# A fused attention and channel-mix kernel: the first unit's softmax done tile by tile under another order list, and part of the token mix moved to ScalarE in later units

## The chip, the cores and the metric

The kernel runs on one core of a Trainium2 chip. The metric is device time in microseconds (us) of one execution. Five engines work side by side, each through its own instructions in order: TensorE (PE, matrix products), VectorE (DVE), ScalarE (ACT), GpSimd (POOL) and SyncE (SP), which here issues all DMA transfers. An engine that waits for a semaphore holds up everything behind it in its own order.

## The reference

Chunked local attention, then a channel mix on its output. All is float32; B, H, S, D = 4, 8, 768, 64, so x has 4 x 768 rows of 512.

```python
# attention, chunks of 32 queries; context 16 left, 8 right, and 8 memory keys
scores = scale * np.matmul(q_c, k_full.transpose(0, 1, 3, 2))
scores = scores - np.max(scores, axis=-1, keepdims=True)
a = np.exp(scores)
a = a / (np.sum(a, axis=-1, keepdims=True) + 1e-09)
out[:, :, c_start:c_end] = np.matmul(a, v_full)
...
# channel mix on x, the attention output as (B, S, 512)
x_prev = np.concatenate([np.zeros((B, 1, D), dtype=np.float32), x[:, :-1, :]], axis=1)
xk = mu_k * x + (1.0 - mu_k) * x_prev
xr = mu_r * x + (1.0 - mu_r) * x_prev
k = np.maximum(xk @ w_k, 0.0)
v = k * k @ w_v
r = 1.0 / (1.0 + np.exp(-(xr @ w_r)))
return (r * v).astype(np.float32)
```

## The kernel before

**Tiling.** The 3072 tokens are 24 tiles of 128 and 12 units of two tiles (256 tokens). A product of the channel mix is made of three matmuls in a rounded float32 format: the operand's high part times the weight's high part, high times low, and low times high. So every operand and every weight is split once into a high part (a rounding copy, `.hi`) and a low part (a subtraction, `.lo`).

**Operations by name.** The program is a set of named operations, put in order by a planner (`Plan.order`, lines 114 to 209). For a unit u: `qk` and `vw` load a tile's inputs (672 and 512 KB), `s` computes the scores of both tiles on TensorE (lines 418 to 433), `max`, `sub`, `exp`, `sum`, `norm` are the softmax (lines 435 to 465) on arrays of 128 x 1024. For a tile t: `t` transposes the weights of attention on TensorE into PSUM, `bd.0` and `bd.1` copy the two halves of partitions into a block-diagonal buffer `aTz` (line 497), `a` multiplies with the values (line 509), `x` copies the result into `xT` (line 524). The tracker of tiles makes `bd.1` wait for `bd.0` where they run on different engines, since both write `aTz`. `mix` forms xk and xr: for unit 0 on TensorE with two diagonal matrices of mu and 1 - mu, which ScalarE makes in `dg` (lines 341 to 348), for later units on VectorE as x_prev + mu (x - x_prev), a subtraction `df` (line 593) and four fused multiply-adds per output (line 603). `h`, `g`, `v` are the three products (lines 654, 630, 630), and from unit 3 on the last product runs in seven blocks (line 961).

**Weights.** A weight chunk `w{i}` arrives as 64-bit words (1024 KB). ScalarE makes its magnitude (`.mag`, line 376), VectorE shifts the low word (`.low`, line 379) and joins them (`.join`, line 383), then come `.hi` and `.lo` (lines 316, 318, 389). Chunks w2 to w5 are w_k, needed by `h`; w0 and w1 are w_r, needed by `g`; w6 to w9 are w_v.

**What sets the order.** A string `FIRST` (lines 47 to 64) lists the operations up to the last `v` block of unit 0 as `name@engine`; the planner takes them in that order. Behind it, it places by itself, from estimated costs and due times (`te_order`, lines 212 to 241), choosing the engine where an operation has a choice. Buffers are rings: `big` has 4 places that hold both `qk` tiles and raw weights, so a transfer may wait until an old tile was read. Where the planned order leaves TensorE idle before unit 0's first `h`, the program puts in products of zeros, `warm` (lines 1085 to 1088), one for each 0.86 us of the planned gap.

Of the kernel before, what the change touches and what calls it, by code (L numbers as in the profile page):

```python
# [52 lines left out]
bd3.1@dve vw3@dma xl0.1@dve w5.load@dma w5.mag@act w0.load@dma s2@pe max2@dve w1.load@dma qk7@dma sub2@dve w5.low@dve
w5.join@dve w0.low@dve exp2@act sum2@dve vw4@dma a2@pe a3@pe x2@act x3@act w5.hi@act w5.lo@dve h0.0@pe h0.1@pe
w1.low@dve w0.mag@act h0.2@pe h0.3@pe w1.mag@act qk6@dma w0.join@dve w0.hi@act relu0.0@act norm2@dve t4@pe bd4.0@act
relu0.1@act sq0.1@act vw5@dma sq0.0@act kh0.0@act t5@pe w0.lo@dve s3@pe g0.0@pe relu0.3@act w1.join@dve w1.hi@dve
relu0.2@act bd4.1@act bd5.1@act sq0.3@act w7.load@dma w7.mag@act bd5.0@act w1.lo@dve g0.1@pe sq0.2@act a4@pe x4@act
df1@dve kh0.1@dve mix1.1@dve xh1.1@dve w8.load@dma w8.mag@act xl1.1@dve w6.load@dma a5@pe x5@act w6.mag@act mix1.0@dve
xh1.0@dve xl1.0@pool sig0.0@act sig0.1@act max3@dve sub3@dve kl0.1@dve w7.low@dve w9.load@dma w9.low@dve w6.low@dve
w7.join@dve kh0.3@act g1.0@pe g1.1@pe h1.0@pe sig1.0@act sig1.1@act w6.join@dve kl0.0@dve kh0.2@act w9.mag@act  # L60
w9.join@dve w6.hi@act kl0.3@dve exp3@act h1.1@pe w6.lo@dve h1.2@pe relu1.1@act sq1.1@act w7.hi@act w8.low@dve
w8.join@dve h1.3@pe relu1.0@act kl0.2@dve w9.hi@act relu1.3@act w7.lo@dve sq1.0@act df2@dve w8.hi@act w8.lo@dve
# [182 lines left out]
def local_attention__then__channel_mix(  # L245
# [162 lines left out]
    def scores(u):  # L408
# [62 lines left out]
        o_s = op(f"s{u}", ("pe", 1.4), f_s, l + [prior.get("s")], new=[s1], use=qs, due=ds)  # L471
        o_m = op(f"max{u}", ("dve", 1.17), f_max, [o_s], new=[m1], use=[s1], due=ds + 4)
        o_b = op(f"sub{u}", ("dve", 1.17), f_sub, [o_m], new=[e], use=[s1, m1], due=ds + 5.5)
        o_e = op(f"exp{u}", ("act", 1.02), f_exp, [o_b], use=[e], table="exp")
        o_u = op(f"sum{u}", ("dve", 1.65, True), f_sum, [o_e], new=[m2], use=[e])
        o_n = op(f"norm{u}", either(dve=(1.14, True), pool=(2.2, True)), f_norm, [o_u], use=[e, m2])
        prior.update(s=o_s)
        return o_n, e
# [661 lines left out]
```

## Time and profile before

| What | Value |
|---|---|
| three runs | 485.79, 399.02 and 399.14 us; median 399.14 us |
| the profiled execution | 398.94 us, of which the span of the profile is 397.2 us |
| TensorE busy | 388.1 us, 98% of the span |
| VectorE busy | 323.2 us, 81% |
| ScalarE busy | 215.2 us, 54% |
| GpSimd busy | 15.9 us, 4% |
| bytes moved by DMA | 46.63 MB |

The first run of the three lies far above the other two, which agree with the profiled execution within 0.2 us. Busy shares are means over stages with different limits: the first 21 us, in which inputs and weights arrive and the first unit's softmax runs, are another regime than the rest.

### The profile page before, as it was taken

What the parts mean: (1) busy time and instruction counts of PE and PEld (TensorE: products, weight loads), DVE (VectorE), ACT (ScalarE), POOL (GpSimd) and SP (SyncE); (2) the same over time, 40 slices, a digit from 0 to 9 for tenths busy, and PEclk for the clock granted to TensorE, in tenths of its full rate; (3) what the DMA queues carried; (4) which work ended last, traced back from release to release, by engine and by line L of the source; (5) the groups of instructions that cost most, each with busy time, mean ns of one, the idle gap of its engine ahead of it and who ended that gap; (6) DMA issues with size and microseconds to landing.
All of it is one profiled execution on the core that took longest, in us unless ns stands there. A gap on an engine that the chain in (4) does not pass through costs nothing.

```text
span 397.2 us, 10852 instructions
## 1 busy us (share of the span) xinstructions
PE 388.1 (98%) x4803; PEld 357.6 (90%) x4803; DVE 323.2 (81%) x561; ACT 215.2 (54%) x340; POOL 15.9 (4%) x14
## 2 busy tenths in 40 slices
PE   7889999999999999999999999999999999999996
PEld 3579889888988989989989989989989999989995
DVE  1888989998789999789879879779779779478446
ACT  1867797714642864457457466357358364344440
POOL 2243020000010000000000000000000000000000
PEclk9999999999999999999999999999999999999999
DMA  8999894011063260142142142142130130100101
GB/s 304 412 352 355 268 362 133 8 69 39 2 229 110 102 246 3 55 151 98 55 138 110 54 174 73 54 148 99 55 109 2 53 108 2 53 2 2 54 0 53
DMA packets 13054, 46.63 MB, mean 117 GB/s; under 512 B 1488, under 2 KB 1872, under 8 KB 12496
## 3 DMA queue, kind: packets, MB, share of 16 engines
q1 hardware_dynamic: 13008, 45.95, 31.9%
q8 instruction: 37, 0.61, 0.6%
q14 instruction: 9, 0.07, 0.1%
HBM read 39.65 MB, written 6.29 MB: 116 GB/s over the span
## 4 chain that ended last, share of the span: by engine, by line
PE 93%; DVE 3%; ACT 2%; DMA 1%; issue 0%; SPq 0%; DVEq 0%
PE ph L654 33%; PE pr L630 17%; PE pv L630 8%; PE pa L961 6%; PE pb L961 6%; PE px L509 6%; PE pc L961 5%; PE s L430 4%; PE pd L961 3%; PE pt L492 3%; PE xf L562 2%; DMA qk<-in_qk_dram 1%; ACT k L346 1%; DVE sm_sb L443 1%; DVE e L447 1%; DVE o L985 0%
## 5 line engine op out<-in xcount | busy, mean ns | idle before, releaser
L654 PE MATMUL ph<-xh,wkh 128*128 128x256 f32 x384 | 106.2, 277 | 0.0
L654 PE MATMUL ph<-xl,wkh 128*128 128x256 f32 x384 | 106.0, 276 | 0.0
L654 PE MATMUL ph<-xh,wkl 128*128 128x256 f32 x384 | 106.0, 276 | 0.0
L654 PEld LDWEIGHTS ph<-xh,wkh 128*128 128x128 f32 x384 | 72.1, 188 | 0.2
L654 PEld LDWEIGHTS ph<-xl,wkh 128*128 128x128 f32 x384 | 72.1, 188 | 0.0
L654 PEld LDWEIGHTS ph<-xh,wkl 128*128 128x128 f32 x384 | 72.1, 188 | 0.0
L742 ACT ACTIVATE k<-ph 128x512 f32<-128x512 f32 x48 | 28.6, 598 | 71.9 <-PE ph L654 71.8
L917 DVE TENSOR_TENSOR khl<-k,khl 128x512 fp32r<-128x512 f32 x63 | 42.2, 687 | 25.4 <-ACT khl L316 24.4
L630 PE MATMUL pr<-wrh,xh 128*128 128x512 f32 x96 | 39.1, 408 | 0.0
L630 PE MATMUL pr<-wrl,xh 128*128 128x512 f32 x96 | 37.6, 392 | 0.0
L630 PE MATMUL pr<-wrh,xl 128*128 128x512 f32 (+1 forms) x108 | 37.6, 366 | 0.0
L316 ACT CAST khl<-k 128x512 fp32r<-128x512 f32 x43 | 26.4, 622 | 7.5 <-PE pb L961 2.5
L630 PE MATMUL pv<-wvh,khl 128*128 128x512 f32 (+1 forms) x97 | 30.3, 389 | 0.0
L749 ACT ACTIVATE k<-k 128x512 f32<-128x512 f32 x47 | 29.5, 632 | 1.3
L509 PEld LDWEIGHTS px<-aTz,vw 128*64 128x64 f32 x768 | 23.4, 138 | 3.4 <-issue 2.4
L509 PE MATMUL px<-aTz,vw 128*64 128x64 f32 x768 | 25.0, 223 | 1.1 <-DVE aTz L318 1.1
L318 DVE CAST khl<-k 128x512 fp32r<-128x512 f32 x32 | 13.1, 423 | 15.6 <-ACT k L749 15.2
L316 ACT COPY aTz<-pt 64x512 f32<-64x512 f32 x34 | 19.1, 580 | 12.0 <-PE pt L492 11.1
L701 ACT ACTIVATE sg<-pr 128x512 f32<-128x512 f32 x24 | 14.3, 599 | 19.4 <-PE pr L630 19.3
L961 PE MATMUL pc<-wtbig,khl 128*128 128x256 f32 x204 | 24.6, 276 | 0.0
L630 PEld LDWEIGHTS pr<-wrh,xl 128*128 128x128 f32 x108 | 20.3, 188 | 4.6
L961 PEld LDWEIGHTS pc<-wtbig,khl 128*128 128x128 f32 x204 | 23.8, 188 | 0.0
(110 smaller groups left out, 757.3 us busy)
## 6 DMA issues: line engine op xcount, KB each, us to landing
qk<-in_qk_dram SPq DMA_DIRECT2D x24, 672.0 KB, 6.1
vw<-in_vw_dram SPq DMA_DIRECT2D x24, 512.0 KB, 4.8
out_dram<-o SPq DMA_DIRECT2D x23, 256.0 KB, 2.1
raw<-in_w_k_dram SPq DMA_DIRECT2D x4, 1024.0 KB, 8.0
raw<-in_w_v_dram SPq DMA_DIRECT2D x4, 1024.0 KB, 6.6
raw<-in_w_r_dram SPq DMA_DIRECT2D x2, 1024.0 KB, 5.9
out_dram<-o SPq DMA_DIRECT2D x2, 128.0 KB, 1.7
id_sb<-in_ident_dram SPq DMA_DIRECT2D x1, 64.0 KB, 6.8
```

The costliest lines, as they stand in the source:

```text
L316: e.copy(dst, src)
L318: e.tensor_copy(dst, src)
L430: nc.tensor.matmul(s5[CHUNK * j : CHUNK * (j + 1), h, c, r, :], q4[z, r, j, :], k3[z, r, STEP * j : STEP * j + NK], start=True, stop=True,)
L492: nc.tensor.transpose(p[:, n * P : (n + 1) * P], e[:, n // 2, c, n % 2, :], id_sb)
L509: nc.tensor.matmul(p3[64 * h : 64 * h + 64, 2 * g : 2 * g + 2, CHUNK * j : CHUNK * j + CHUNK], v[:, g, h, j, :], a[:, h, g, j, :], start=True,
L630: nc.tensor.matmul(p[:, a : a + step], x, w[:, a : a + step], start=start, stop=stop and a + step == DM)
L654: nc.tensor.matmul(z, w, x[:, k], start=start, stop=stop)
L701: nc.scalar.activation(T["sg", u][:, c * DM : (c + 1) * DM], T["pr", u, c], AF.Sigmoid)
L742: e.activation(r, T["ph", u, f], AF.Relu)
L749: e.activation(q, q, AF.Square)
L917: e.tensor_sub(T["al", u, name], src, T["ah", u, name].bitcast(F32))
L961: nc.tensor.matmul(p, l[:, i], r[i], start=i + k == 0, stop=i == FT // 2 - 1 and k == 2)
```

## The change

Three edits.

1. **The first unit goes tile by tile.** For u = 0 the scores of the second tile go into two PSUM buffers of the tag `tp` instead of the second half of the `s` buffer, and `s`, `max`, `sub`, `exp`, `sum`, `norm` exist once for each tile; those of the second tile are named with a `b` (`s0b`, `max0b`, ...). `t0` waits for the first tile's `norm0`, `t1` for `norm0b`. In all units the mask of an edge tile is written by one memset for each head half, where it was one for both.
2. **Another list `FIRST`.** It covers the same stretch, up to the last `v` block of unit 0. It also names other engines for some operations: `norm0`, `w7.lo`, `kl0.3` and `kl1.2` go to GpSimd, `norm1` and `xl1.0` leave it.
3. **From unit 3 on, ScalarE makes (1 - mu) x_prev** (`old`, four activations of 128 x 256 for each of the two outputs), and VectorE adds mu x with its four fused operations. The subtraction `df` is gone there.

The list begins so (the rest of it is shown by the rows further down):

```diff
-qk1@dma qk0@dma s0@pe max0@dve sub0@dve mu@dma w3.load@dma w3.low@dve w3.mag@act w3.join@dve exp0@act sum0@dve id@dma
-norm0@dve dg0@act dg1@act qk2@dma qk3@dma s1@pe t0@pe t1@pe bd0.0@act vw1@dma w3.hi@dve w3.lo@pool bd1.1@act vw0@dma
...
+qk0@dma s0@pe qk1@dma max0@dve sub0@dve exp0@act s0b@pe max0b@dve mu@dma id@dma sum0@dve norm0@pool qk3@dma qk2@dma
+w3.load@dma dg1@act vw0@dma vw1@dma w2.load@dma sub0b@dve exp0b@act sum0b@dve norm0b@dve dg0@act w3.mag@act s1@pe
...
```

The rest of the code, cut to its core:

```diff
+        split = u == 0
+        parts = [[c] for c in range(QPU)] if split else [range(QPU)]
...
+        def f_s(cs):
+            if cs[0] == 0:
+                T["s", u] = ps("s", f"s{u}", QPU)
+            else:
+                for h in range(2):
+                    T["s", u, cs[0], h] = ps("tp", f"s{u}_{h}")
...
-                nc.vector.memset(s5[0:CHUNK, :, c, :, 0:LEFT], NEG)
...
+                for h in range(2):
+                    if qts[ts[c]][1] == 0:
+                        nc.vector.memset(room(h, c)[0:CHUNK, :, 0:LEFT], NEG)
...
+        for n, cs in enumerate(parts):
...
+            o_s = op(f"s{u}{v}", ("pe", 1.4 * z), on(f_s), [l[c] for c in cs] + [prior.get("s")], new=[s1] if first else t1, use=[qs[c] for c in cs], due=ds)
...
+            o_e = op(f"exp{u}{v}", ("act", 1.02 * z), on(f_exp), [o_b], use=[e], table="exp")
...
+            norms += [o_n] * len(cs)
...
-        o_t = op(f"t{t}", ("pe", 0.45), f_t, [o_n, o_id, prior.get("t")], new=[s2], use=[e], due=dt)
+        o_t = op(f"t{t}", ("pe", 0.45), f_t, [o_n[c], o_id, prior.get("t")], new=[s2], use=[e], due=dt)
...
+        if u >= FAST:
+            for m in (0, 1):
+                fs = Slot("x4", [0, 1])
...
+                    f = T["xf", u, m] = sb(fs, [P, KT, UTOK], f"xf{u}_{m}")
+                    for k in range(KT):
+                        nc.scalar.activation(
+                            f[:, k], T["xT", u][:, k, :UTOK], AF.Copy, scale=mu_sb[:, m + 2, k : k + 1]
+                        )
...
+                        nc.vector.scalar_tensor_tensor(
+                            f[:, k], T["xT", u][:, k, 1 : 1 + UTOK], mu_sb[:, m, k : k + 1], f[:, k], ALU.mult, ALU.add
+                        )
```

**How the order moved, first place: SyncE's transfers and ScalarE up to the first `bd`.** A number behind `raw` is the weight chunk, behind `qk` and `vw` the tile; the last number in a name is the buffer's own. SyncE before, from its first transfer on:

```order
L416 DMA qk1_101<-in_qk_dram 128x1344
L416 DMA qk0_103<-in_qk_dram 128x1344
L333 DMA mu_sb_65<-in_mu_dram 128x8
L360 DMA raw3_179<-in_w_k_dram 128x1024
L332 DMA id_sb_64<-in_ident_dram 128x128
L416 DMA qk2_209<-in_qk_dram 128x1344
L416 DMA qk3_211<-in_qk_dram 128x1344
L486 DMA vw1_295<-in_vw_dram 128x1024
L486 DMA vw0_300<-in_vw_dram 128x1024
L360 DMA raw2_304<-in_w_k_dram 128x1024
L360 DMA raw4_362<-in_w_k_dram 128x1024
```

SyncE of the change, the same stretch:

```order
L418 DMA qk0_101<-in_qk_dram 128x1344
L418 DMA qk1_139<-in_qk_dram 128x1344
L335 DMA mu_sb_65<-in_mu_dram 128x8
L334 DMA id_sb_64<-in_ident_dram 128x128
L418 DMA qk3_189<-in_qk_dram 128x1344
L418 DMA qk2_191<-in_qk_dram 128x1344
L362 DMA raw3_193<-in_w_k_dram 128x1024
L529 DMA vw0_204<-in_vw_dram 128x1024
L529 DMA vw1_206<-in_vw_dram 128x1024
L362 DMA raw2_208<-in_w_k_dram 128x1024
L362 DMA raw4_301<-in_w_k_dram 128x1024
```

Tile 0 now comes first, and the first weight chunk w3 moved from the fourth place to the seventh; the first eleven transfers are the same eleven.

ScalarE before, from its first work to the copy of the second tile (`mag3` is `w3.mag`, `e0` is `exp0`, `k20` and `k21` the diagonals of `dg0` and `dg1`, `aTz` are `bd`, `xT0` are `x0` and `x1`):

```order
L376 ACTIVATE mag3_182<-raw3_179 128x1024
L455 ACTIVATE e0_176<-e0_176 128x1024
L343 ACTIVATE mu_sb_65<-mu_sb_65 128x4
L346 ACTIVATE k20_80<-id_sb_64,mu_sb_65 128x128 x8
L343 ACTIVATE mu_sb_65<-mu_sb_65 128x4
L346 ACTIVATE k21_81<-id_sb_64,mu_sb_65 128x128 x8
L316 COPY aTz0_78<-pt0_284 64x16x32
L316 COPY aTz1_79<-pt1_289 64x16x32 x2
L521 COPY xT0_340<-zero_sb_84 128x4
L316 COPY xT0_340<-px0_306 128x4x128
```

ScalarE of the change:

```order
L485 ACTIVATE e0_144<-e0_144 128x512
L345 ACTIVATE mu_sb_65<-mu_sb_65 128x4
L348 ACTIVATE k21_81<-id_sb_64,mu_sb_65 128x128 x8
L485 ACTIVATE e0_144<-e0_144 128x512
L345 ACTIVATE mu_sb_65<-mu_sb_65 128x4
L348 ACTIVATE k20_80<-id_sb_64,mu_sb_65 128x128 x8
L378 ACTIVATE mag3_226<-raw3_193 128x1024
L318 COPY aTz0_78<-pt0_296 64x16x32
L318 COPY aTz1_79<-pt1_304 64x16x32 x2
L565 COPY xT0_358<-zero_sb_84 128x4
L318 COPY xT0_358<-px0_312 128x4x128
L318 COPY xT0_358<-px1_339 128x4x128
```

The first exponential no longer stands behind `w3.mag`, the diagonals lie around the second exponential, `w3.mag` stands directly ahead of the first `bd`, and `x1` came over from VectorE.

**Second place: VectorE from the normalization of unit 1 on.** `raw4` and `mag4` are `w4.low` and `w4.join`, `xl0_0` is `xl0.0` (two halves), `aTz0` is `bd2.1`, `aTz1` a half of tile 3. VectorE before:

```order
L379 TENSOR_SCALAR raw4_362<-raw4_362 128x1024
L576 TENSOR_TENSOR xl0_0_391<-xf00_351,xh0_0_369 128x512
L576 TENSOR_TENSOR xl0_0_391<-xf01_356,xh0_0_369 128x512
L383 SCALAR_TENSOR_TENSOR mag4_367<-mag4_367,raw4_362 128x1024
L318 COPY aTz0_78<-pt2_386 64x16x32
L318 COPY aTz1_79<-pt3_405 64x16x32
```

VectorE of the change:

```order
L381 TENSOR_SCALAR raw4_301<-raw4_301 128x1024
L496 TENSOR_TENSOR e1_332<-e1_332,sm_sb_82 128x1024
L385 SCALAR_TENSOR_TENSOR mag4_399<-mag4_399,raw4_301 128x1024
L620 TENSOR_TENSOR xl0_0_411<-xf00_363,xh0_0_402 128x512
L620 TENSOR_TENSOR xl0_0_411<-xf01_368,xh0_0_402 128x512
L320 COPY aTz0_78<-pt2_406 64x16x32
```

`norm1` came over from GpSimd and stands directly ahead of `w4.join`, which moved in front of `xl0.0`. On ScalarE the high part of w4 moved in front of the copy for tile 2; before:

```order
L316 CAST xh0_1_399<-xf11_380 128x512
L316 COPY aTz0_78<-pt2_386 64x16x32
L316 COPY aTz1_79<-pt3_405 64x16x32
L316 CAST wkh2_68<-mag4_367 128x1024
L376 ACTIVATE mag5_422<-raw5_420 128x1024
```

and in the change:

```order
L318 CAST xh0_1_480<-xf11_378 128x512
L318 CAST wkh2_68<-mag4_399 128x1024
L318 COPY aTz0_78<-pt2_406 64x16x32
L318 COPY aTz1_79<-pt3_490 64x16x32 x2
L567 COPY xT1_514<-xT0_358 128x4
```

So `bd2.0` (the first `aTz0` row) now comes behind `w4.hi`, and both halves of tile 3 are ScalarE's. On TensorE the only moves up to unit 0's first `h` are that `s2` stands between `t2` and `t3`, and that 7 products of zeros stand where 9 stood (two ahead of `s0`, three behind `s0b`, one ahead of each of `a0` and the first `mix`).

## Rows read from the trace of the kernel before

**Rows 1.** Busy time of each engine by stage (stretch in us, its length, then busy us and instructions in parentheses for each engine, the granted clock as a share of full speed, the DMA engines' busy share and GB/s): up to the first `mix`, from there to TensorE's last matmul block, and one later unit.

```profile
0.00:21.44 21.44, 16.21 (x347) 9.47 (x347) 11.90 (x16) 12.12 (x28) 4.65 (x9) 1.00 0.92 362
...
21.44:390.68 369.24, 369.21 (x4435) 345.67 (x4436) 307.71 (x537) 203.11 (x313) 11.28 (x5) 1.00 0.29 104
...
157.68:188.05 30.37, 30.37 (x407) 28.99 (x407) 26.10 (x45) 17.15 (x27) 0.00 (x0) 1.00 0.29 99
```

**Rows 2.** Waits of TensorE over the whole span: who waited, for whom, us in total, times, longest us.

```profile
PE s L430 <- DMA qk<-in_qk_dram: 1.9, 2, 1.1
PE xf L562 <- DVE xT L318: 1.1, 1, 1.1
PE px L509 <- DVE aTz L318: 1.1, 1, 1.1
```

**Rows 3.** The chain of work that ended last, in order of time up to unit 0's first `h`: start us, us, what.

```profile
1.18 5.48 DMA qk<-in_qk_dram
...
6.70 1.50 PE s L430 x91
...
9.73 1.24 DVE e L447
...
10.99 1.06 ACT e L455
...
12.14 2.34 ACT k L346 x8
...
14.57 2.34 ACT k L346 x8
16.91 0.48 ACT aTz L316
...
17.42 0.69 DVE aTz L318
...
19.47 1.23 DVE e L447
20.70 0.61 DVE xT L318
...
21.44 7.15 PE xf L562 x32
28.59 0.87 PE pt L492 x8
29.46 1.41 PE s L430 x89
30.87 2.02 PE px L509 x64
32.89 11.08 PE ph L654 x96
```

**Rows 4.** Single DMA issues, each the answer for a stretch that holds one issue: KB, us from issue to landing. In this order, issued at 0.75 us (`qk1`), 8.21 (`qk3`), 8.58 (`vw1`), 9.07 (`vw0`) and 12.95 (w4). The last row is a stretch as in rows 1, with all engines' data rate at its end.

```profile
qk<-in_qk_dram SPq DMA_DIRECT2D x1, 672.0 KB, 4.2
...
qk<-in_qk_dram SPq DMA_DIRECT2D x1, 672.0 KB, 6.0
...
vw<-in_vw_dram SPq DMA_DIRECT2D x1, 512.0 KB, 6.9
...
vw<-in_vw_dram SPq DMA_DIRECT2D x1, 512.0 KB, 7.7
...
raw<-in_w_k_dram SPq DMA_DIRECT2D x1, 1024.0 KB, 8.8
...
2.50:21.44 18.94, 14.77 (x346) 8.63 (x344) 11.73 (x15) 10.83 (x27) 2.81 (x2) 1.00 1.01 405
```

**Rows 5.** TensorE in order of time: start us, us, line, operation, tiles, shape and count (a float32 matmul stands as two records), and in brackets the idle time before.

```profile
1.06 4.58 PE L1088 MATMUL warm<-zero_sb 128*128 128x512 f32 x6 [1.06 <-DVE zero_sb L305]
...
8.11 4.56 PE L1088 MATMUL warm<-zero_sb 128*128 128x512 f32 x10
12.60 0.86 PE L430 MATMUL s<-qk 64*32 64x64 f32 x64
```

**Rows 6.** ScalarE and VectorE in order of time, for durations by shape: `w4.mag`, a half of `xh0.0`, then `x1` and `xl0.0` (two halves).

```profile
21.86 1.15 ACT L376 ACTIVATE mag<-raw 128x1024 f32<-128x1024 f32 x1
23.44 0.59 ACT L316 CAST xh<-xf 128x512 fp32r<-128x512 f32 x1 [0.43 <-PE xf L562]
...
20.61 0.68 DVE L318 COPY xT<-px 128x512 f32<-128x512 f32 x1
...
25.32 1.27 DVE L576 TENSOR_TENSOR xl<-xf,xh 128x512 fp32r<-128x512 f32 x2
```

**Rows 7.** VectorE and GpSimd in order of time around GpSimd's second and third work of unit 0: `w2.join`, `w4.join`, then `w2.lo` and `w4.lo` on GpSimd.

```profile
22.00 1.23 DVE L383 SCALAR_TENSOR_TENSOR mag<-mag,raw 128x1024 uint32<-128x1024 uint32 x1
...
26.51 1.73 DVE L383 SCALAR_TENSOR_TENSOR mag<-mag,raw 128x1024 uint32<-128x1024 uint32 x1
...
27.12 3.35 POOL L389 TENSOR_TENSOR wkl<-mag,wkh 128x1024 fp32r<-128x1024 f32 x1
31.93 2.39 POOL L389 TENSOR_TENSOR wkl<-mag,wkh 128x1024 fp32r<-128x1024 f32 x1 [1.46 <-ACT wkh L316]
```

**Rows 8.** Groups of instructions, for the later units: the subtraction `df` with its count and its durations in ns (min/median/max), and a form on ScalarE of the size of `old` (busy us, mean ns | idle before).

```profile
L593 DVE TENSOR_TENSOR df<-xT x11: 1216/1218/1225, 48.1 to 354.1; 128x1024 f32<-128x1024 f32 x11
...
L316 ACT CAST wtbig<-wz 128x256 fp32r<-128x256 f32 x7 | 2.6, 402 | 1.5 <-DVE wz L862 1.4
```

More of the change, by code (lines that the diff above doesn't have):

```diff
@@ L53 @@
[L53 to L62, printed above, removed]
@@ L63 @@
-relu1.2@act sq1.3@act mix2.1@dve w9.lo@dve v0.0@pe v0.1@pe v0.2@pe sq1.2@act v0.3@pe
+qk0@dma s0@pe qk1@dma max0@dve sub0@dve exp0@act s0b@pe max0b@dve mu@dma id@dma sum0@dve norm0@pool qk3@dma qk2@dma
+w3.load@dma dg1@act vw0@dma vw1@dma w2.load@dma sub0b@dve exp0b@act sum0b@dve norm0b@dve dg0@act w3.mag@act s1@pe
+t0@pe w4.load@dma bd0.0@act t1@pe w3.low@dve bd0.1@dve a0@pe w3.join@dve w3.hi@dve max1@dve sub1@dve qk5@dma
+w3.lo@pool bd1.0@act bd1.1@act a1@pe qk4@dma x0@act x1@act mix0.0@pe mix0.1@pe w2.low@dve w2.mag@act w2.join@dve
@@ new lines @@
+vw2@dma exp1@act vw3@dma sum1@dve w5.load@dma w4.low@dve norm1@dve w4.mag@act w4.join@dve xh0.0@act w2.hi@act t2@pe
+xl0.0@dve s2@pe w2.lo@pool xh0.1@act w4.hi@act bd2.0@act w0.load@dma bd2.1@dve w1.load@dma t3@pe bd3.1@act bd3.0@act
+a2@pe x2@act xl0.1@dve qk6@dma a3@pe max2@dve h0.0@pe w4.lo@pool w5.mag@act w5.low@dve x3@act sub2@dve w5.join@dve
+h0.1@pe h0.2@pe w0.low@dve vw4@dma exp2@act w0.mag@act sum2@dve w1.low@dve w5.hi@act w5.lo@dve h0.3@pe qk7@dma
+w1.mag@act w0.join@dve w0.hi@act norm2@dve t4@pe w1.join@dve t5@pe w0.lo@dve relu0.1@act df1@dve relu0.0@act sq0.0@act
@@ L64 @@
+df2@dve w8.mag@act sq1.0@act w9.low@dve w6.lo@dve h1.2@pe h1.3@pe relu1.2@act relu1.1@act w9.mag@act relu1.3@act
+sq1.2@act v0.0@pe w8.join@dve w9.join@dve sq1.3@act w8.hi@act mix2.1@dve v0.1@pe exp3@act w9.hi@act w8.lo@dve v0.2@pe
+kh1.0@dve kl1.0@dve sq1.1@act w9.lo@dve kh1.1@act kl1.1@dve xh2.1@act xl2.1@dve mix2.0@dve kh1.2@act kl1.2@pool
+v0.3@pe
 """
@@ L470, in scores, with on @@
         l = [op(f"qk{t}", ("dma", 1.68), lambda t=t, x=x: f_load(t, x), [], new=[x]) for t, x in zip(ts, qs)]
[L471 to L478, printed above, removed]
+        norms, z = [], 0.55 if split else 1.0
+        t1 = [Slot("tp") for _ in range(2 * split)]
+        for n, cs in enumerate(parts):
+            def on(f, cs=cs):
+                return lambda: f(cs)
+            v, first = "b" * n, n == 0
+            o_s = op(f"s{u}{v}", ("pe", 1.4 * z), on(f_s), [l[c] for c in cs] + [prior.get("s")], new=[s1] if first else t1, use=[qs[c] for c in cs], due=ds)
+            o_m = op(f"max{u}{v}", ("dve", 1.17 * z), on(f_max), [o_s], new=[m1] * first, use=[s1, *t1, m1], due=ds + 4)
+            o_b = op(f"sub{u}{v}", ("dve", 1.17 * z), on(f_sub), [o_m], new=[e] * first, use=[s1, *t1, m1, e], due=ds + 5.5)
+            o_e = op(f"exp{u}{v}", ("act", 1.02 * z), on(f_exp), [o_b], use=[e], table="exp")
+            o_u = op(f"sum{u}{v}", ("dve", 1.65 * z, True), on(f_sum), [o_e], new=[m2] * first, use=[e, m2])
+            o_n = op(
+                f"norm{u}{v}", either(dve=(1.14 * z, True), pool=(2.2 * z, True)), lambda g, cs=cs: f_norm(g, cs), [o_u],
+                use=[e, m2],
+            )
+            norms += [o_n] * len(cs)
+            prior.update(s=o_s)
+        return norms, e
     def attention(t, o_n, e):
@@ L582, in mixed, with both, f_hi, f_lo @@
             mix[0, m] = (o_h, o_l, hs, ls)
+    def both(u, m, o_d, fs):
+        def f_hi(e):
+            h = T["xh", u, m] = split_x(f"xh{m}", f"xh{u}_{m}", m)
+            copy(e, h, T["xf", u, m])
+        def f_lo(e):
+            l = T["xl", u, m] = split_x(f"xl{m}", f"xl{u}_{m}", m)
+            e.tensor_sub(l, T["xf", u, m], T["xh", u, m].bitcast(F32))
+        hs, ls = Slot(f"xh{m}"), Slot(f"xl{m}")
+        o_h = op(f"xh{u}.{m}", either(act=(1.0,), dve=(0.61, True)), f_hi, [o_d], new=[hs], use=[fs])
+        o_l = op(f"xl{u}.{m}", either(dve=(1.14, True), pool=(2.4, True)), f_lo, [o_h], new=[ls], use=[fs, hs])
+        mix[u, m] = (o_h, o_l, hs, ls)
     def prep(u):
```

104 lines of the change are left out of this document (61 added, 43 removed).

## The prediction

> **What bounds the kernel now.** I read the busy time by stage first. TensorE is busy for 369.21 of the 369.24 us between 21.44 and 390.68 us, at a granted clock of 1.00, and for only 16.21 of the 21.44 us before, some of that with products of zeros [rows 1]. So whatever the other engines do later is hidden by TensorE as long as nothing comes too late for it, and the change adds or removes no product behind the first `mix`. Next the waits of TensorE: after its start it waits only for `qk`, for `bd` (1.1 us) and for `x1` (1.1 us) [rows 2], all before 21.44. Time can be won only by letting unit 0's `mix` start earlier, and it can be lost at any later place where data then misses its turn.
>
> The chain up to 21.44 says what held `mix` [rows 3]. Tile 0 was the second transfer and landed at 6.65. Scores, max, sub and the exponential ran on whole units until 12.05; ScalarE then made both diagonals (2.34 us each) before it reached `bd0.0` at 16.91; VectorE followed with `bd0.1` until 18.11, then took max and sub of unit 1 ahead of `x1` (20.70 to 21.30).
>
> **The first tiles: when `a0` can start.** I follow the changed order with durations from the rows. Tile 0 is now the first transfer; the first landed at 0.75 + 4.2 = 4.95 [rows 4]. Its 32 score products take 0.86 us [rows 5], until 5.9. Half-size max and sub are not in the trace: they cost more than nothing and less than the whole 1.24 [rows 3]; the nearest row, a 128x512 read from PSUM, has 0.68 [rows 6], which I take. With the memsets they end near 7.6, a half exponential (0.59, as the 128x512 cast [rows 6]) near 8.2. On ScalarE come `dg1` (2.4), `exp0b` (0.6), `dg0` (2.4): it is free at 13.6. In the old order that point was 16.9.
>
> But ScalarE's next work is `w3.mag`, and `bd0.0` stands behind it. So what ends last is likely the landing of w3, now the seventh transfer. Before, the seventh to land was `qk3`, at 8.21 + 6.0 = 14.2 [rows 4], behind the same bytes: four `qk`, mu, the identity and w3. That is my upper bound. The lower one is the data rate: these are 3.87 MB, and at 405 GB/s from about 2.5 us [rows 4] they have passed by 12.1. I take 13.9, near the upper end, since both `vw` and w2 stand directly behind w3 as they stood behind `qk3`.
>
> From 13.9: `w3.mag` 1.15 [rows 6] to 15.05, `bd0.0` about 0.55 (0.48 and its overlap with the next [rows 3]) to 15.6, `bd0.1` 0.69 to 16.3, `a0` at 16.4. Its `vw0`, the eighth, should land at 15.5 as the eighth did (8.58 + 6.9), and `vw1`, the ninth, at 16.8 (9.07 + 7.7) [rows 4], before `a1` at 17.4. `a0` and `a1` took 18.21 to 20.29, so they end at 18.5; `x1`, now on ScalarE and directly behind `x0`, 0.6; with the 0.14 us to `mix` [rows 3] it starts at 19.2 instead of 21.44. **Gain here 2.2 us**: about 1.8 from `a0` and 0.4 because max and sub of unit 1 no longer stand ahead of `x1`. With w3 at 12.2, ScalarE's 13.6 rules instead and `mix` starts at 18.8; with 14.2, at 19.5.
>
> `norm0` on GpSimd costs nothing: a 128x512 there is not longer than the 2.39 of the double size [rows 7], so from 9.3 it ends before 11.7, and `t0` has until 16. If that cover went, each us of it would delay `a0` by one. The same holds for the second tile's softmax: `norm0b` ends near 13, three us before `bd1` needs `t1`.
>
> **What is late next.** From 19.2, `mix` takes 7.15, `t2`, `s2`, `t3` together 0.87 + 1.41 [rows 3]; TensorE is free for `a2` at 28.65. On ScalarE, the last half of `xh0.1` waits for the last `mix` product (26.5) and ends at 27.1, then come `w4.hi` (1.05) and only then `bd2.0`, to 28.6; `bd2.1` on VectorE, 0.69, ends at 29.3. So **`a2` waits about 0.7 us**, a wait that the old order does not have: `bd2.0` stood ahead of `w4.hi`, and TensorE had no idle time there. After 2.02 us of `a2` and `a3`, `h0` starts at 31.4 instead of 32.89 [rows 3]. Net **1.5 us**.
>
> Behind that I see no new wait. The weights for `h0.0` (w2, w3) are split by 28; w4's low part on GpSimd ends near 31, over 4 us before `h0.2`. w5 for `h0.3` is the tightest: all its steps shift with TensorE except its landing, which the same sixteen transfers set; a delay of one us would cost up to one us.
>
> **Later units.** The removed `df` is 1.22 us of VectorE in nine of its eleven units [rows 8]; the eight fused operations per unit stay. The 72 new activations of 128x256 are not in the trace; they cost more than nothing and, by the 128x256 cast at 402 ns [rows 8] with a few tens of ns of overlap, some 0.3 to 0.5 us each. I take 0.4: 3.2 us per unit of 30.37 us, in which ScalarE is busy for 17.15 and VectorE for 26.10 [rows 1]. Both stay under the unit's length, and TensorE's zero idle time there hides the cost as well as the relief: I put both at nothing. The added memsets (about 0.15 us in edge units) fall under it too.
>
> **Sum.** 398.94 of the profiled execution - 2.2 + 0.7 = 397.4; the median of the runs shown is 0.2 higher, so **397.6 us**. This is 0.4% less; a difference under 2% is about what a measurement of this kernel cannot tell from no change.
>
> **Rivals.**
> *GpSimd takes VectorE's turn (slower).* Before, `w4.join` took 1.73 instead of 1.23, beginning while GpSimd worked and ending 1.1 us after; and `w2.lo`, begun while the join ran, took 3.35 instead of 2.39 [rows 7]. So one of the two waited for the other. In the change, `w2.lo` asks at about 25 (w4 lands at 12.95 + 8.8 = 21.75 [rows 4], then `w4.mag`, two casts, `w2.hi`), while `norm1` runs on VectorE (24.3 to 25.5), and `w4.join` stands directly behind it. If GpSimd gets in between them, the join starts 2.4 us later, and `w4.hi`, `bd2.0`, `bd2.1` and `a2` with it: `a2` starts at 31.4 instead of 29.3 and the time is 397.6 + 2.1 = 399.7, slower than before; 400.3 if it gets ahead of `norm1` as well and holds up `t2`. It decides at one point, who goes first at 25.5. For it: in the row before, the join that waited got its turn at the end of GpSimd's operation, ahead of GpSimd's next one. Against: VectorE begins its next instruction without a gap.
> The Trainium skill ("SBUF — State Buffer", section on SBUF's two separate sides) calls the port pair that the two engines share an exclusive lock, which whoever starts first holds for its whole instruction. The row's 1.73 and 3.35 agree. The page does not say who follows, so by it alone the sum could be either 397.6 or 399.7.
> *w3 lands later, and the gain is gone.* If w3 shares the rate with the two `vw` behind it and lands with them at 15.4, `mix` starts at 20.7 and `h0` at 32.9: 399.1, no change. Against: `qk3` stood as w3 does now and landed at 14.2.
> *TensorE's clock falls.* The change has two products of zeros less and longer gaps around them. The first six records of `warm` took 4.58 us and a later ten 4.56 [rows 5]: the clock was at the lower level, 1.2 GHz, and rose to 2.4 after some us of work. If it fell before `mix`, its 7.15 us would take up to 14.3: up to 404.7. Against: gaps of 1.1 us before `a0` and `mix` left it at 1.00 [rows 1], and the new one before `a0` is about 2 us.
> *The later units decide.* If VectorE bounded them, 9 x 1.22 = 11 us would be won (386.6); if `old` held up ScalarE's release of PSUM, 9 x 3.2 = 29 us would be lost (427). The zero idle time of TensorE and 13 us per unit of idle ScalarE speak against both.
>
> **How the numbers follow.** Forecast 0.56 (its own range 396.7 to 398.3: w3 between 12.2 and 14.2, the wait of `a2` between nothing and 1.1); GpSimd first 0.26 (399.2 to 400.3); w3 late 0.10 (398.4 to 399.4); clock 0.03; later units 0.01 won and 0.02 lost; 0.02 unplaced. From 396.6 to 400.3 lie the first three, 0.92 less what their own sizes may miss, about 0.83. Faster by over 2% (under 391.2): 0.01. Slower by over 2% (over 407.1): 0.02. Within: 0.97.
>
> **What would show it.** Right: tile 0's scores near 5.0, `w3.mag` beginning when w3 lands between 12 and 14.3, `a0` at 16.4, `mix` at 19.2, a wait of `a2` for VectorE's `aTz`, `h0` at 31.4, then no idle TensorE until about 389.2. Wrong: `w4.join` starting over 27 or taking over 3 us beside `w2.lo` (first rival); `w3.mag` at 15 (second); a first `mix` over 8 us (third); TensorE idle in a later unit, behind `old` on ScalarE (last).

## The result, and the profile after

The changed kernel took 401.63 us (median of 9 executions, 399.75 to 403.76) against 399.14 us before; the ratio is 1.0059, with a 95% interval from 1.0041 to 1.0076. So it is about 0.6% slower, within 2%, and the interval lies clear of no change; 397.6 us and a small gain were forecast. The profiled execution took 401.29 us, its span 399.5 us.

The times of the nine executions go with TensorE's mean granted clock: the one at 1.000 took 399.75 us, those at 0.991 and 0.992 took 402.87 and 403.76, the other six, at 0.993 to 0.996, lie from 400.3 to 401.91. That mean takes in the end of the span too, where TensorE has no work left: in the profiled execution the granted clock is 0.50 from 398 us on.

The stages first (columns as in [rows 1]: length, busy time and instructions of each engine, granted clock, DMA share, GB/s). I cut the stretch between the first `mix` and 60 us finer, since the busy share there is not what it was.

```profile
0.00:21.44 21.44, 17.44 (x354) 10.94 (x355) 12.42 (x24) 13.30 (x30) 5.70 (x10) 1.00 0.92 368
...
28.50:31.40 2.90, 0.00 (x0) 0.00 (x0) 2.48 (x5) 2.25 (x4) 1.16 (x1) 1.00 0.44 88
31.40:32.50 1.10, 1.08 (x36) 1.08 (x38) 1.10 (x2) 0.53 (x2) 1.10 (x1) 0.99 1.05 432
32.50:34.00 1.50, 1.50 (x36) 1.50 (x30) 1.30 (x4) 1.38 (x2) 0.10 (x1) 0.50 1.02 418
34.00:36.00 2.00, 2.00 (x15) 1.88 (x12) 2.00 (x4) 0.84 (x2) 0.00 (x0) 0.53 1.04 426
36.00:38.00 2.00, 2.00 (x20) 2.00 (x18) 2.00 (x4) 1.96 (x2) 0.00 (x0) 1.00 1.00 409
...
60.00:390.68 330.68, 330.68 (x3847) 310.54 (x3846) 265.62 (x490) 198.54 (x335) 14.88 (x7) 1.00 0.23 78
```

Three things are to be seen. TensorE is busy for 17.44 us of the first 21.44 instead of 16.21 [rows 1], so the start did get earlier. Between 28.5 and 31.4 it does nothing at all, where the order of before had no idle time [rows 3]. And from 32.5 to about 36 its clock is at 0.50 to 0.53, the lower of its two levels, 1.2 instead of 2.4 GHz. From 60 us to 390.68 there is not one idle tenth of a us: what cost time lies before.

TensorE in order of time says where (start us, us, line, operation, tiles, shape, count, and in brackets the idle time before and what ended it):

```profile
16.00 2.09 PE L553 MATMUL px<-aTz,vw 128*64 128x64 f32 x64 [1.10 <-DVE aTz L320]
18.01 1.13 PE L1157 MATMUL warm<-zero_sb 128*128 128x512 f32 x2
18.97 7.07 PE L606 MATMUL xf<-xT,k 128*128 128x256 f32 x32
...
27.83 0.66 PE L536 MATMUL pt<-id_sb,e 128*128 128x128 f32 x4
31.42 2.83 PE L553 MATMUL px<-aTz,vw 128*64 128x64 f32 x64 [2.94 <-DVE aTz L320]
34.19 0.58 PE L723 MATMUL ph<-xh,wkh 128*128 128x256 f32 x1
...
36.00 0.28 PE L723 MATMUL ph<-xh,wkl 128*128 128x256 f32 x1
```

`a0` starts at 16.00 instead of 18.21 and `mix` at 18.97 instead of 21.44 [rows 3]: 2.47 us won. Then `a2` waits 2.94 us for `bd2.1`, `a2` and `a3` take 2.83 us instead of 2.02 [rows 3], and `h0` starts at 34.19 instead of 32.89: 1.3 us lost.

What `bd2.1` waited for is read on VectorE, GpSimd and ScalarE, each in order of time: `norm1`, `w4.join` and `bd2.1`; `w2.lo`; `w4.hi` and `bd2.0` with `bd3`.

```profile
24.55 1.21 DVE L496 TENSOR_TENSOR e<-e,sm_sb 128x1024 f32<-128x1024 f32 x1
25.69 3.40 DVE L385 SCALAR_TENSOR_TENSOR mag<-mag,raw 128x1024 uint32<-128x1024 uint32 x1
...
30.67 0.69 DVE L320 COPY aTz<-pt 64x512 f32<-64x512 f32 x1 [0.39 <-ACT aTz L318]
...
24.67 3.32 POOL L391 TENSOR_TENSOR wkl<-mag,wkh 128x1024 fp32r<-128x1024 f32 x1 [4.30 <-ACT wkh L318]
...
29.11 1.04 ACT L318 CAST wkh<-mag 128x1024 fp32r<-128x1024 f32 x1 [2.45 <-DVE mag L385]
30.07 1.77 ACT L318 COPY aTz<-pt 64x512 f32<-64x512 f32 x3
```

The two long rows belong together. `w2.lo` asks at 24.67 while `norm1` runs, and takes 3.32 us instead of 2.36 to 2.39: by these lengths it waits until `norm1` is over, near 25.7, and works until 27.99. `w4.join`, which by its row begins right behind `norm1`, takes 3.40 us instead of 1.23 [rows 7]: it does nothing until 27.99 and then its 1.1 us. ScalarE waits 2.45 us for the join, makes `w4.hi`, and only then `bd2.0`.

### The profile page after: what moved, and what is told of

Its sections match the earlier page's. It is cut to its first block, busy times and chain, and to the rows that moved or that the text cites. A ratio compares the mean times of both kernels' runs of the same rounds, so it can differ in the third digit from the quotient of the medians.

```text
span 399.5 us, 10927 instructions
## 1 busy us (share of the span) xinstructions
PE 388.8 (97%) x4799; PEld 358.7 (90%) x4799; DVE 317.7 (80%) x570; ACT 241.1 (60%) x406; POOL 26.3 (7%) x19
## 4 chain that ended last, share of the span: by engine, by line
PE 92%; DVE 5%; ACT 2%; issue 1%; DVEq 0%; ACTq 0%
PE ph L723 33%; PE pr L699 17%; PE pv L699 8%; PE pa L1030 6%; PE pb L1030 6%; PE px L553 6%; PE pc L1030 5%; PE s L457 3%; PE pd L1030 3%; PE pt L536 2%; DVE mag L385 1%; ACT k L348 1%; PE warm L1157 1%; DVE sm_sb L472 0%; DVE e L481 0%
## 5 line engine op out<-in xcount | busy, mean ns | idle before, releaser
L811 ACT ACTIVATE k<-ph 128x512 f32<-128x512 f32 x48 | 28.5, 598 | 82.7 <-PE ph L723 75.9
L986 DVE TENSOR_TENSOR khl<-k,khl 128x512 fp32r<-128x512 f32 x61 | 40.9, 688 | 25.8 <-ACT khl L318 24.6
L653 ACT ACTIVATE xf<-xT,mu_sb 128x256 f32<-128x256 f32 x72 | 30.0, 497 | 1.8 <-DVE xT L320 1.5
L660 DVE SCALAR_TENSOR_TENSOR xf<-xT,mu_sb,xf 128x256 f32<-128x256 f32 x72 | 29.9, 476 | 0.0
L553 PE MATMUL px<-aTz,vw 128*64 128x64 f32 x768 | 25.8, 227 | 4.0 <-DVE aTz L320 4.0
L318 ACT CAST xh<-xf 128x1024 fp32r<-128x1024 f32 (+1 forms) x20 | 19.0, 953 | 15.3 <-DVE xf L660 14.3
L320 DVE CAST khl<-k 128x512 fp32r<-128x512 f32 x36 | 14.7, 424 | 16.7 <-ACT k L818 15.3
L318 ACT CAST khl<-k 128x512 fp32r<-128x512 f32 x39 | 24.1, 619 | 5.0 <-PE pb L1030 2.4
```

What stands on the lines that cost most here:

```text
L318: e.copy(dst, src)
L320: e.tensor_copy(dst, src)
L553: nc.tensor.matmul(p3[64 * h : 64 * h + 64, 2 * g : 2 * g + 2, CHUNK * j : CHUNK * j + CHUNK], v[:, g, h, j, :], a[:, h, g, j, :], start=True,
L653: nc.scalar.activation(f[:, k], T["xT", u][:, k, :UTOK], AF.Copy, scale=mu_sb[:, m + 2, k : k + 1])
L660: nc.vector.scalar_tensor_tensor(f[:, k], T["xT", u][:, k, 1 : 1 + UTOK], mu_sb[:, m, k : k + 1], f[:, k], ALU.mult, ALU.add)
L811: e.activation(r, T["ph", u, f], AF.Relu)
```

## The experiments

My theory after the result has two steps. First, GpSimd's `w2.lo` gets the turn between `norm1` and `w4.join`; that delays the join by 2.2 us, and through `w4.hi`, `bd2.0` and `bd2.1` it delays `a2`. Second, the wait of 2.94 us lets TensorE's clock fall, which costs another 1.5 us or so. The rivals are the third edit (`old` on ScalarE), the contention as such wherever it is, and a clock that falls for another reason. Each median stands beside the kernel before on the same chip, which took 399.24 us with e1 to e4, 399.20 with e5 to e8, and 399.16 with e9 and e10. In e2 and e5 to e10, products of zeros are put in only up to `t2`, which keeps the planner from adding one behind it. Beyond `FIRST` the planner's own order shifts a little in some of them.

**e4, the third edit undone.**

```diff
-        if u >= FAST:
+        if False:
             for m in (0, 1):
                 fs = Slot("x4", [0, 1])
```

> The third edit undone: later units subtract df on VectorE again and ScalarE makes no old. Theory: both are hidden under TensorE, so the time stays at 401.6 within 0.5 us, with the same wait of 2.94 us ahead of a2. Rival (later units cost the time): 399 or less, with the wait ahead of a2 unchanged.

It took 401.39 us (400.06 to 401.65), ratio 1.0060 [1.0046, 1.0073]: the later units are not where the time goes. The profiled execution is the one of 400.06 us, and it is worth a look. TensorE in order of time, `a2` with `a3`, then the first product of `h0` and the ninth:

```profile
31.72 2.08 PE L553 MATMUL px<-aTz,vw 128*64 128x64 f32 x64 [2.94 <-DVE aTz L320]
33.74 0.38 PE L723 MATMUL ph<-xh,wkh 128*128 128x256 f32 x1
...
34.78 0.28 PE L723 MATMUL ph<-xh,wkl 128*128 128x256 f32 x1
```

The stretch of `a2` and `a3`, columns as in the stages:

```profile
31.70:33.70 2.00, 1.98 (x64) 1.95 (x64) 1.80 (x5) 1.31 (x4) 1.20 (x1) 1.00 1.02 414
```

The wait is again 2.94 us, but here the clock stayed at 1.00 and `a2` with `a3` took 2.08 us. This execution had a mean clock of 1.000, the other four 0.996, and those took 401.18 to 401.65, 1.1 to 1.6 us more. No trace shows where their clock fell; behind the wait is the likely place, as in the changed kernel. So the fall seems to follow the wait in most executions, and does not in all.

**e3, TensorE kept busy ahead of the wait.** Two products of zeros are put ahead of the scores of unit 2; they are overwritten by the scores.

```diff
+            if u == 2:
+                for _ in range(2):
+                    nc.tensor.matmul(T["s", u][:, :512], zero, zeros, start=True, stop=True)
             for c in cs:
                 a = T["qk", ts[c]]
```

> Two products of zeros (1.9 us of TensorE) ahead of the scores of unit 2; nothing else changes. Theory: a2 still starts near 31.4, since it waits for bd2.1; but TensorE is idle for 1.0 us instead of 2.94 ahead of it, so the clock stays at 1.00 and a2 with a3 takes 2.05 us instead of 2.83, h0 starts near 33.5 and its first products are at full speed: 399.5 to 400.0. Rival (the clock falls for another reason than the idle time): 401.6, with the granted clock again under 1.00 between 31 and 36 us.

It took 400.18 us (399.69 to 401.35), ratio 1.0026 [1.0013, 1.0040]; 1.45 us less than the changed kernel, although TensorE has more work. TensorE in order of time:

```profile
32.24 2.08 PE L556 MATMUL px<-aTz,vw 128*64 128x64 f32 x64 [1.21 <-DVE aTz L320]
```

The same stretch with its clock:

```profile
32.20:34.20 2.00, 1.96 (x64) 1.95 (x64) 1.79 (x5) 1.31 (x4) 1.22 (x1) 1.00 1.01 412
```

`a2` starts as late behind `mix` as in the changed kernel (12.44 us against 12.45; in this execution `mix` began at 19.80), but the idle time ahead of it is 1.21 us, and the clock stayed. This separates the two shares: about 1.5 us of the time is the clock, the rest of the loss the wait itself. One execution of the seven, 401.35 us at a clock of 1.000, is not explained by this.

**e1, `w2.lo` on VectorE, so that nothing stands between `norm1` and `w4.join`.**

```diff
-xl0.0@dve s2@pe w2.lo@pool xh0.1@act w4.hi@act bd2.0@act w0.load@dma bd2.1@dve
+xl0.0@dve s2@pe xh0.1@act w4.hi@act bd2.0@act w0.load@dma bd2.1@dve w2.lo@dve
```

> Theory (port turn, then the clock): without GpSimd's w2.lo between them, w4.join follows norm1 at once and takes 1.23 us instead of 3.40; a2 starts near 29.1 after a wait of 0.6 to 0.7 us instead of 2.94, the granted clock stays at 1.00 in 31 to 36 us, a2 and a3 take 2.05 us, and h0 starts near 31.2. That takes 2.2 us (wait) and 1.9 us (clock) off 401.6: 397.5. VectorE now carries w2.lo itself (about 1.2 us) ahead of w5's split, so a wait of up to 1.2 us may appear within h0: 397.5 to 398.7. Rival (the later units' old on ScalarE costs the time): no more than 0.5 us under 401.6.

It took 399.78 us (399.18 to 400.64), ratio 1.0014 [1.0000, 1.0028]. The mechanism came as expected, the time did not. The four joins by their durations in ns (min/median/max):

```profile
L385 DVE SCALAR_TENSOR_TENSOR mag<-mag,raw x4: 1215/1222/1226, 16.7 to 36.8; 128x1024 uint32<-128x1024 uint32 x4
```

VectorE's `w2.lo`, then TensorE, in order of time:

```profile
29.99 2.28 DVE L391 TENSOR_TENSOR wkl<-mag,wkh 128x1024 fp32r<-128x1024 f32 x1
...
30.02 2.09 PE L553 MATMUL px<-aTz,vw 128*64 128x64 f32 x64 [0.77 <-DVE aTz L320]
...
42.01 0.39 PE L723 MATMUL ph<-xh,wkl 128*128 128x256 f32 x1 [0.94 <-DVE wkl L391]
```

No join is long any more, the wait of `a2` is 0.77 us, just what the prediction had, and the clock stayed at 1.00. But `w2.lo` now waits in its turn, 2.28 us instead of 1.22, beside `w4.lo` on GpSimd, and w5's low part behind it on VectorE comes 0.94 us late for `h0`. `mix` also began 0.77 us later in this execution (19.74). Taking GpSimd's work away removed the loss and put part of it elsewhere.

**e9, `w2.hi` and `w2.lo` moved behind `xh0.1`,** so that GpSimd asks after the join has begun.

```diff
-w4.join@dve xh0.0@act w2.hi@act t2@pe xl0.0@dve s2@pe w2.lo@pool xh0.1@act w4.hi@act
+w4.join@dve xh0.0@act t2@pe xl0.0@dve s2@pe xh0.1@act w2.hi@act w2.lo@pool w4.hi@act
```

> The changed kernel with w2.hi (ScalarE) and w2.lo (GpSimd) moved behind xh0.1, everything else as it was. Theory (who asks while the other engine works gets the turn at its end): w2.lo now asks near 27.7, after w4.join has begun, so w4.join takes 1.23 us and not 3.4; bd2.0 now has w2.hi and w4.hi ahead of it (2.1 us of ScalarE), so a2 starts near 30.3 after a wait of 1.6 us, and the clock stays: 398.6 to 399.6. Rival (w4.join is slow whenever GpSimd has work near it): the join over 2.5 us and a2 at 32 or later: 401.5 to 403.

It took 398.32 us (397.89 to 399.31), a little under the range expected, ratio 0.9982 [0.9969, 0.9994]: two names moved within the list take back 3.3 us. `w4.join`, then `w2.lo` with `w4.lo`, then `a2`:

```profile
25.86 1.22 DVE L385 SCALAR_TENSOR_TENSOR mag<-mag,raw 128x1024 uint32<-128x1024 uint32 x1
...
27.86 4.71 POOL L391 TENSOR_TENSOR wkl<-mag,wkh 128x1024 fp32r<-128x1024 f32 x2 [7.32 <-ACT wkh L318]
...
29.99 2.08 PE L553 MATMUL px<-aTz,vw 128*64 128x64 f32 x64 [1.33 <-DVE aTz L320]
```

The same operations run on the same engines; only the moment at which GpSimd asks is another. The join takes 1.22 us, and `a2` waits 1.33 us although ScalarE now has two casts ahead of `bd2.0`.

**e5, the join ahead of `norm1`,** to see which of two operations waits.

```diff
-w4.low@dve norm1@dve w4.mag@act w4.join@dve xh0.0@act
+w4.low@dve w4.mag@act w4.join@dve norm1@dve xh0.0@act
```

> w4.join ahead of norm1 on VectorE, all else as in the changed kernel. Theory (a GpSimd operation that asks while VectorE works gets the turn at the end of VectorE's instruction): w2.lo asks near 24.7 to 25.8, during w4.join, and runs when that ends; it is now norm1 that takes about 3.4 us, w4.join takes 1.23, TensorE waits some 2.6 us for norm1 ahead of t2 instead of 2.94 ahead of a2, and the time is 401 to 402.5. Rival (the join as an operation of its own kind is slow beside GpSimd, or it was chance): norm1 takes 1.2 us, t2 waits under 0.5 us, a2 under 0.5 us, 398 to 399.

It took 401.85 us (400.59 to 402.54), ratio 1.0065 [1.0050, 1.0079]. The time came as the theory had it, the row did not (`w4.join` and `norm1`, then `w2.lo`, then `t2`):

```profile
24.92 3.38 DVE L385 SCALAR_TENSOR_TENSOR mag<-mag,raw 128x1024 uint32<-128x1024 uint32 x1
28.22 1.21 DVE L496 TENSOR_TENSOR e<-e,sm_sb 128x1024 f32<-128x1024 f32 x1
...
24.86 2.35 POOL L391 TENSOR_TENSOR wkl<-mag,wkh 128x1024 fp32r<-128x1024 f32 x1 [4.32 <-ACT wkh L318]
...
29.49 0.66 PE L536 MATMUL pt<-id_sb,e 128*128 128x128 f32 x4 [3.28 <-DVE e L496]
```

The stretch behind that wait:

```profile
31.00:33.00 2.00, 2.00 (x76) 1.50 (x60) 1.89 (x4) 0.00 (x0) 0.83 (x1) 0.50 0.86 346
```

`w2.lo` started 0.06 us ahead of the join and took its plain 2.35 us; the join waited for it, and `norm1` was late in full. So it shows that the later one waits, but it is no test of who gets a turn between two of VectorE's instructions. TensorE waited 3.28 us for `norm1`, and its clock fell behind that wait too. Over all runs, a mean clock of 0.996 or less stands in 17 of the 20 executions of the three kernels with a wait of about 3 us (the changed one, e4 and e5), and in 9 of the 74 of the other experiments.

**e2, the copies of `bd2` and `bd3` ahead of `w4.hi` on ScalarE,** `bd2.1` with them, which was VectorE's. The contention stays; what hangs on it does not.

```diff
-w2.lo@pool xh0.1@act w4.hi@act bd2.0@act w0.load@dma bd2.1@dve w1.load@dma t3@pe bd3.1@act bd3.0@act
+w2.lo@pool xh0.1@act bd2.0@act bd2.1@act w0.load@dma w1.load@dma t3@pe bd3.1@act bd3.0@act w4.hi@act
...
-                n = 0 if ("ph", 0, 0) in T else int((o.start - busy - 0.1) / (0.86 if busy else 1.72))
+                n = 0 if ("pt", 2) in T else int((o.start - busy - 0.1) / (0.86 if busy else 1.72))
```

> Theory: w4.join still takes 3.4 us beside w2.lo, but bd2 and bd3, all four on ScalarE and ahead of w4.hi, no longer stand behind it: a2 starts right after t3 near 28.5 with a wait under 0.3 us, the clock stays at 1.00, h0 starts near 30.6, and the time is 396.5 to 397.5; w4's split, now behind, has until about 36. Rival (the contention itself costs TensorE time wherever it is): 399 or more. Rival (later units): about 401.6.

It took 398.06 us (397.75 to 399.10), ratio 0.9976 [0.9967, 0.9985]: faster than both kernels. VectorE's `w4.join`, then TensorE's `a2` and its longest later wait:

```profile
26.04 3.40 DVE L385 SCALAR_TENSOR_TENSOR mag<-mag,raw 128x1024 uint32<-128x1024 uint32 x1
...
28.76 1.15 PE L553 MATMUL px<-aTz,vw 128*64 128x64 f32 x32
...
40.31 0.39 PE L723 MATMUL ph<-xh,wkl 128*128 128x256 f32 x1 [0.42 <-DVE wkl L391]
```

The join still takes 3.40 us and costs `a2` nothing: it starts without a wait, and `a3` waits 0.23 us for ScalarE's copies. The rival that contention costs wherever it is falls. That the time is 0.6 us above the upper end expected has two reasons in the rows: `mix` began at 19.32 in this execution instead of 18.97, and `h0` waits 0.42 us for w5's low part.

**e7, e2 with `x1` on VectorE as before the change;** the planner fills one product of zeros more into the gap ahead of `mix`.

```diff
-x0@act x1@act mix0.0@pe
+x0@act x1@dve mix0.0@pe
```

> The kernel with bd2 and bd3 first (398.1), but x1 on VectorE as before the change. The prediction gave x1's move 0.4 us of the gain at the start: 398.5 by that. Rival: VectorE takes max1 and sub1 until about 20.4 whatever a1 does, so x1 ends at 21 and mix starts near 21.0 to 21.4 as before the change, 1.8 us later: 399.8 to 400.2, and the earlier a0 is worth nothing without x1's move.

It took 399.64 us (399.37 to 400.36), ratio 1.0010 [1.0000, 1.0020]: 1.58 us more than e2. `sub1` and `x1` on VectorE, then `mix`:

```profile
19.43 1.23 DVE L481 TENSOR_TENSOR e<-s,sm_sb 128x1024 f32<-128x1024 f32 x1
20.57 0.68 DVE L320 COPY xT<-px 128x512 f32<-128x512 f32 x1
...
21.39 7.14 PE L606 MATMUL xf<-xT,k 128*128 128x256 f32 x32 [1.29 <-DVE xT L320]
```

`mix` starts at 21.39, practically where it did before the change (21.44): the earlier `a0` and `a1` are worth nothing as long as `x1` stands behind `max1` and `sub1`.

**e6, e8 and e10, further in the direction that e2 showed.** e6 puts `bd0.0` and `bd0.1` ahead of `w3.mag`; e8 takes, besides, w5's split ahead of the softmax of unit 2; e10 is e6 with `w2.hi` and `w2.lo` behind `bd2`.

```diff
-dg0@act w3.mag@act s1@pe t0@pe w4.load@dma bd0.0@act t1@pe w3.low@dve bd0.1@dve a0@pe
+dg0@act s1@pe t0@pe bd0.0@act bd0.1@dve w3.mag@act w4.load@dma t1@pe w3.low@dve a0@pe
...
-sub2@dve w5.join@dve h0.1@pe h0.2@pe w0.low@dve vw4@dma exp2@act w0.mag@act sum2@dve w1.low@dve w5.hi@act w5.lo@dve
+w5.join@dve sub2@dve h0.1@pe h0.2@pe w0.low@dve vw4@dma w5.hi@act exp2@act w0.mag@act w5.lo@dve sum2@dve w1.low@dve
...
-w2.hi@act t2@pe xl0.0@dve s2@pe w2.lo@pool xh0.1@act bd2.0@act bd2.1@act
+t2@pe xl0.0@dve s2@pe xh0.1@act bd2.0@act bd2.1@act w2.hi@act w2.lo@pool
```

> The kernel with bd2 and bd3 first (398.1), and bd0.0 and bd0.1 ahead of w3's split on their engines. Theory (in the changed kernel a0 waits for w3's landing and w3.mag through bd0.0): a0 starts when vw0 has landed, near 15.5, instead of 16.0 to 16.8, mix near 18.5 instead of 19.3, and the time is 397.2 to 397.6; w5's split may come up to 0.6 us late for h0, then 397.6 to 398.0. Rival (vw0 lands no earlier than w3 plus 1.5 us, so nothing is won): 398.1.

> As the kernel with bd0 early, and w5.join ahead of sub2, w5.hi ahead of exp2, w5.lo ahead of sum2. Theory: h0's wait for w5's low part (0.4 us with bd2 first) is gone, t4 may wait up to 0.4 us for the softmax of unit 2 instead: 397.0 to 397.6. Rival (it only moves the wait): as the kernel with bd0 early.

> The kernel with bd0 early and bd2, bd3 first (398.0), and w2.hi, w2.lo behind bd2. Theory: w4.join takes 1.23 us, so VectorE, which is busy for 96% of 36 to 60 us there, gets 2.2 us back, h0's wait for w5's low part (0.4 us) is gone, and h0 starts within 0.3 us of where it did (31.0): 397.3 to 397.8. Rival (w2.lo, now near 29 to 31.3, comes too late for h0.0): 398.0 to 398.6.

e6 took 398.04 us (ratio 0.9972 [0.9962, 0.9982]), e8 397.89 us (0.9976 [0.9963, 0.9988]), e10 397.61 us (397.20 to 398.14; 0.9956 [0.9940, 0.9971]). e6 and e8 lie above what their theories expected (e8's rival, that the wait only moves, came true), e10 within. e10 is the lowest of all, but its interval overlaps those of e6 and e8. TensorE in e6, in order of time:

```profile
18.64 7.07 PE L605 MATMUL xf<-xT,k 128*128 128x256 f32 x32
25.91 0.66 PE L535 MATMUL pt<-id_sb,e 128*128 128x128 f32 x4 [0.20 <-DVE e L495]
...
30.97 0.38 PE L722 MATMUL ph<-xh,wkh 128*128 128x256 f32 x1
...
40.05 0.38 PE L722 MATMUL ph<-xh,wkl 128*128 128x256 f32 x1 [0.42 <-DVE wkl L390]
```

TensorE in e8, the one wait in its `h0` and up to `t4`:

```profile
42.39 1.06 PE L535 MATMUL pt<-id_sb,e 128*128 128x128 f32 x8 [0.47 <-DVE e L495]
```

TensorE's first `h0` in e10, and then the stretch from 36 to 60 us:

```profile
31.31 0.38 PE L722 MATMUL ph<-xh,wkh 128*128 128x256 f32 x1
```

```profile
36.00:60.00 24.00, 24.00 (x323) 21.65 (x322) 22.27 (x29) 19.53 (x29) 2.83 (x2) 1.00 0.77 289
```

In e6 `mix` starts 0.68 us earlier than in e2, and the time is the same: `t2` now waits for VectorE's `norm1`, so that `h0` starts only 0.26 us earlier, and the wait of 0.42 us for VectorE stands in `h0` as in e2. e8 removes that one and finds one of 0.47 us at `t4`, for VectorE's `norm2`. Only e10, in which `w4.join` takes 1.22 us, has neither: between 36 and 60 us TensorE is never idle. But its `h0` began 0.34 us later than in e6, and `w5.join` waits there in its turn (2.30 us). So with an earlier start it is VectorE that comes late; that the 2.2 us of `w4.join` are what it lacks fits these rows, and the times do not show it (397.77 us in the profiled execution of e6, 397.75 in that of e10).

## Why the prediction was wrong

**The start was right, its shares were not.** `mix` was forecast for 19.2 and came at 18.97; in the other profiled executions with the changed start it lies between 19.14 (e5, e9) and 19.80 (e3). ScalarE took `w3.mag` at 13.58, where the prediction let w3 land at 13.9, and `a0` came at 16.00 instead of 16.4. But "about 1.8 from `a0` and 0.4 because max and sub of unit 1 no longer stand ahead of `x1`" does not hold as two separate shares: without the move of `x1` nothing is left of the gain at `mix` (e7).

**The step that failed is the wait of `a2`,** "about 0.7 us". It measured 2.94. It was worked out with a join that follows `norm1` at once; e1, where that is so, has 0.77. The first rival named the mechanism, the place and `a2` at 31.4 (31.42 measured), and gave it a chance of 0.26. The argument against it was that VectorE begins its next instruction without a gap. By the start of its row it does, and that is no turn: the instruction stands there for 2.2 us and waits. The row that spoke for the rival, the join of before that got its turn when GpSimd's operation ended [rows 7], was the same turn seen from the other side and deserved more than it got.

**The clock was priced at the wrong place.** The third rival let it fall ahead of `mix`, behind gaps of 1 to 2 us; there it stayed at 1.00. (The lower level that the prediction reads from the first products of zeros [rows 5] is one of durations alone: the granted clock of that stretch is 1.00 as well.) It fell behind the 2.94 us that the first rival brings. The two rivals were treated as alternatives, and the one sets off the other. The cost by the rows: `a2` and `a3` 0.75 us more (2.83 against 2.08 in e4), and the first eight products of `h0` 1.81 us (34.19 to 36.00) where e4, at full speed, took 1.04 (33.74 to 34.78). That is 1.5 us, as e3 gave back. The sum, for the profiled execution: 397.4 + 2.1 (31.42 instead of 29.3) + 1.5 = 401.0, against 401.29 measured; 0.3 us stay open.

**The later units were right.** The 72 activations of `old` take 30.0 us, 3.3 per unit where 3.2 was estimated (busy us, mean ns of one, then the idle time before):

```profile
L653 ACT ACTIVATE xf<-xT,mu_sb 128x256 f32<-128x256 f32 x72 | 30.0, 497 | 1.8 <-DVE xT L320 1.5
```

TensorE is never idle there, and e4 shows no difference. **w5 as the tightest of `h0`'s weights** was right as well: it is the wait of 0.42 us in e2 and e6, though what made it late was VectorE's queue and not a landing.

## What to carry to other kernels

Where two engines hold each other up, as VectorE and GpSimd do here, an order list is not enough: ask at which moment each one asks, and price the case in which the one that waits goes next, however closely the other's instructions follow each other. Then look at what hangs on the loser: with the same 3.4 us join the kernel takes 401.63 us with `bd2` behind it and 398.06 us with `bd2` ahead of it (e2). A wait on TensorE of the length seen here (2.94 and 3.28 us) should be priced with a fall of the clock behind it, and rivals that can set each other off belong in one sum.
